# Writing 1/Q and its product with Q into the PSUM bank of h, in an attention, rational-MLP and expert kernel

## The chip, the cores and the metric

One core of one Trainium2 chip runs the whole program. The metric is device time in microseconds (us). The kernel before took 926.52 us, the median of 3 runs (925.81 to 928.81).

## The reference, cut to what matters

Three layers follow each other: causal attention with a window of 128 and a linear bias (4 batches, 8 heads, 576 tokens, 64 per head), a dense layer whose activation is a quotient of polynomials, and a top-1 mixture of 8 experts with ReLU. All is fp32. The change touches the quotient alone:

```python
h = x @ w_in                                  # 2304 tokens, 512 -> 2048
P = a[0] + a[1]*h + a[2]*h2 + a[3]*h3
Q = 1.0 + abs(b[0])*abs(h) + abs(b[1])*h2
g = P / (Q + 1e-06)
x = g @ w_out                                 # 2048 -> 512
```

## The kernel before

The 2304 tokens go in nine chunks of 256. For a chunk, `chunk_a` (L811) walks the 2048 columns of h in eight slots of 256 columns. This text counts these slots through the program, from 0 to 71; slots 0 to 7 are chunk 0. In a slot TensorE (PE) makes h with `up` (L478): two weight tiles with 12 matmuls each, three products (L482, L483, L484) for each quarter of the 512 inputs, because a value is carried as a rounded high part and the rest. They fill one tile `h_ps` of 128x512 fp32, a whole PSUM bank; its pool `ps_h` has two buffers, and all eight banks of PSUM are given out. So slot j+2 writes the bank that slot j wrote.

`rational` (L496) makes g of a slot on three other engines. ScalarE (ACT) takes ah = |h| (L503), u = c3 h + c2 (L504) and qq = b2 ah + b1 (L505); GpSimd (POOL) multiplies qq by ah (L508); ACT makes r0 = 1/Q as exp(-ln(qq + 1)) (L509, L510). VectorE (DVE) multiplies u by h (L511), adds c1 and multiplies by h (L512), adds c0 and multiplies by r0 (L515), makes (qq + 1) r0 (L518), and takes one Newton step (L521). ACT rounds the result to gh (L524) and POOL makes the rest gl (L525). u, qq and r0 have two buffers each, in SBUF. L503, L504, L511 and L512 are the only instructions that read the bank of h.

`down` (L486) multiplies gh and gl by the second half of the weights: 12 matmuls (L491, L492, L493) that add into two PSUM banks over a chunk. It runs two slots late (`LAG = 2`), so that PE's order is up(j+2), an attention piece, down(j), another attention piece, up(j+3):

```python
            run_slot(h)
            h_ps = ps_h.tile([P, 2, T], F32, name="h_ps")
            for i in range(2):
                up(w_res[2 * j + i], *xs[c], h_ps[:, i, :])
            run_slot(h + 1)
            if len(pend) >= LAG:
                flush()
            g = rational(h_ps)
```

`run_slot` issues pieces of the attention of a later chunk and of the routing of an earlier one, by a table that `plan_attention` and `routed` fill: scores (L340), transposes of the probabilities (L373), their product with v (L392), and on ACT and DVE the softmax, the rounding and splitting of q, k and x (L310 to L315, L399, L400), and copies out of PSUM (L378).

The order on each engine is a scheduler's, which follows a model of the time. From chunk 1 to chunk 8 PE is excepted (`tc.manual_schedule(engines={mybir.EngineType.PE})`): there it runs in the order in which the code is written. In chunk 0, whose slots also convert the weights, and in the expert stage the scheduler orders PE too. The tag `r0` of the pool `ep` also serves two setup tiles and a part of the expert weights in `load_split`.

Of the kernel before, what the change touches and what calls it, by code (L numbers as in the profile page):

```python
# [11 lines left out]
F32 = mybir.dt.float32  # L12
# [5 lines left out]
AF = mybir.ActivationFunctionType  # L18
ALU = mybir.AluOpType
# [4 lines left out]
P = 128  # L24
T = 256
# [18 lines left out]
def attention_rational_moe_kernel(  # L44
# [11 lines left out]
    nc = tc.nc  # L56
# [18 lines left out]
    ep = ctx.enter_context(tc.tile_pool(name="ep", bufs=2))  # L75
# [15 lines left out]
    co = const.tile([P, 6], F32, name="co")  # L91
# [3 lines left out]
    qc = const.tile([P, 1], F32, name="qc")  # L95
# [15 lines left out]
        out=upper, in_=ones, pattern=[[1, P]], compare_op=ALU.is_gt, fill=0.0,  # L111
# [11 lines left out]
    for h in range(H):  # L123
        sl = 2.0 ** (-8.0 * (h + 1) / H)
        nc.vector.tensor_scalar(
            out=bm[:, h, :], in0=rel, scalar1=-sl * D ** 0.5, scalar2=None, op0=ALU.mult
        )
        nc.gpsimd.affine_select(
            out=bm[:, h, :], in_=bm[:, h, :], pattern=[[-1, 2 * W]], compare_op=ALU.is_ge,
# [3 lines left out]
            out=bm[:, h, :], in_=bm[:, h, :], pattern=[[1, 2 * W]], compare_op=ALU.is_gt,  # L133
# [12 lines left out]
    def small_ps(i, n):  # L146
# [8 lines left out]
        out=tab.rearrange("(p r) c -> p (r c)", p=P), in_=fill.rearrange("p r c -> p (r c)")  # L155
# [340 lines left out]
    def rational(h_ps):  # L496
        u = ep.tile([P, 2, T], F32, name="u")
        ah = ahp.tile([P, 2, T], F32, name="ah")
        qq = ep.tile([P, 2, T], F32, name="qq")
        r0 = ep.tile([P, 2, T], F32, name="r0")  # L500
        gh = ep.tile([P, 2, T], F32R, name="gh", bufs=3)
        gl = ep.tile([P, 2, T], F32R, name="gl", bufs=3)
        nc.scalar.activation(out=ah, in_=h_ps, func=AF.Abs)  # L503
        nc.scalar.activation(out=u, in_=h_ps, func=AF.Identity, scale=co[:, 3:4], bias=co[:, 2:3])  # L504
        nc.scalar.activation(  # L505
            out=qq, in_=ah, func=AF.Identity, scale=babs[:, 1:2], bias=babs[:, 0:1]
        )
        nc.gpsimd.tensor_tensor(out=qq, in0=qq, in1=ah, op=ALU.mult)  # L508
        nc.scalar.activation(out=r0, in_=qq, func=AF.Ln, bias=qc)  # L509
        nc.scalar.activation(out=r0, in_=r0, func=AF.Exp, scale=-1.0)  # L510
        nc.vector.tensor_tensor(out=u, in0=u, in1=h_ps, op=ALU.mult)  # L511
        nc.vector.scalar_tensor_tensor(  # L512
            out=u, in0=u, scalar=co[:, 1:2], in1=h_ps, op0=ALU.add, op1=ALU.mult
        )
        nc.vector.scalar_tensor_tensor(  # L515
            out=u, in0=u, scalar=co[:, 0:1], in1=r0, op0=ALU.add, op1=ALU.mult
        )
        nc.vector.scalar_tensor_tensor(  # L518
            out=qq, in0=qq, scalar=qc, in1=r0, op0=ALU.add, op1=ALU.mult
        )  # L520
        nc.vector.scalar_tensor_tensor(  # L521
            out=u, in0=qq, scalar=2.0, in1=u, op0=ALU.subtract, op1=ALU.mult, reverse0=True
        )
        nc.scalar.copy(gh, u)  # L524
        nc.gpsimd.tensor_tensor(out=gl, in0=u, in1=gh.bitcast(F32), op=ALU.subtract)  # L525
        return gh, gl
# [277 lines left out]
    def chunk_a(c, att):  # L804
        for j in range(NF1 // 2):
            h = 16 * c + 2 * j
            if c == 0:
                convert(2 * j + 2 + LEAD)
# [8 lines that stand above are left out]
            then = 16 * (c + 1) + 5 if c + 1 < NCH else None  # L817
            pend.append((j, NF1 // 2, partial(routed, c, then), w_res[2 * j:2 * j + 2], *g))
            if j % 2 == 0:
                next(att, None)  # L820
            if c == NCH - 1 and j == JE:
                pick_early()
                early.append(prep(None))
            if c == NCH - 1 and j == JE + 2:
                early.append(turn(early.pop()))
# [63 lines left out]
```

## Time and profile before

| | before |
|---|---|
| median of 3 runs | 926.52 us |
| the profiled execution | 929.39 us |
| its span | 927.7 us |
| mean granted clock of TensorE | 0.967 |
| PE matmul, busy | 843.2 us (91%) |
| DVE, busy | 697.0 us (75%) |
| ACT, busy | 623.3 us (67%) |
| POOL, busy | 438.7 us (47%) |

Busy time is the time in which an engine executes; matmuls are pipelined, so that one of 128x256 shows some 290 ns while the next begins 120 ns after it. Idle time counts only on the engine that sets the end. The program has four stretches: the start with the attention of chunk 0 (to 69 us), slots 0 to 7 (69 to 123 us), slots 8 to 71 (123 to 656 us), and the experts, where PE is busy throughout (700 to 900 us).

### The profile page before, as it was taken

Reading aid. Unit: us, or ns where it says so; the run is one execution under the profiler, and the core shown is the slowest. Engines: PE = TensorE matmul, PEld = TensorE weight load, DVE = VectorE, ACT = ScalarE, POOL = GpSimd, SP = SyncE. Lnnn points to the kernel's source line nnn. Section 1 sums busy time; section 2 is a strip of 40 time slices with the busy share of each in tenths; the row PEclk is TensorE's granted clock in tenths of the full one; section 3 lists DMA queues with packets and bytes.
Section 4 is the critical chain, followed back from the end, with each engine's and each line's share of the span. In section 5 each row is a group of like instructions: output and inputs, shape, how many; then the busy total and the mean of one; then the engine's idle time right before and its main releaser. Section 6 shows DMA issues by size and latency. Waiting matters only on the chain. (4 is left out here: it accounts for less than half of the span.)

```text
span 927.7 us, 16232 instructions
## 1 busy us (share of the span) xinstructions
PE 843.2 (91%) x5550; PEld 727.5 (78%) x5550; DVE 697.0 (75%) x1415; ACT 623.3 (67%) x1300; POOL 438.7 (47%) x385
## 2 busy tenths in 40 slices
PE   4669998899899899989999999998969999999994
PEld 2348787778778788878788888887759999999993
DVE  7899997768998888987998988757646875555510
ACT  7999777667678678678778787764627755555510
POOL 3004354355455455454555464535547865555500
PEclk9999999889999999999999999998979999999998
DMA  8851213122122122212113121001448976668300
GB/s 320 288 196 46 82 42 86 44 47 81 43 54 86 37 66 69 61 44 69 49 45 92 38 68 39 1 23 47 115 143 306 316 245 228 227 227 273 125 6 20
DMA packets 69959, 101.88 MB, mean 110 GB/s; under 512 B 14705, under 2 KB 47345, under 8 KB 68082
## 3 DMA queue, kind: packets, MB, share of 16 engines
q1 hardware_dynamic: 64658, 86.11, 29.4%
q0 software_dynamic: 5216, 14.70, 4.5%
q8 instruction: 45, 0.74, 0.3%
q14 instruction: 40, 0.33, 0.1%
HBM read 91.13 MB, written 10.17 MB: 109 GB/s over the span
## 5 line engine op out<-in xcount | busy, mean ns | idle before, releaser
L482 PE MATMUL h_ps<-x,w 128*128 128x256 f32 x896 | 259.6, 291 | 7.9 <-ACT w L219 4.4
L483 PE MATMUL h_ps<-x,w 128*128 128x256 f32 x896 | 258.3, 288 | 0.5 <-DVE x L400 0.5
L484 PE MATMUL h_ps<-x,w 128*128 128x256 f32 x896 | 258.1, 288 | 0.1
L493 PE MATMUL y_ps<-w,gl 128*128 128x512 f32 x448 | 181.7, 409 | 13.3 <-POOL gl L525 13.1
L491 PE MATMUL y_ps<-w,gh 128*128 128x512 f32 x448 | 187.0, 417 | 3.3 <-ACT gh L524 3.2
L508 POOL TENSOR_TENSOR qq<-qq,ah 128x512 f32<-128x512 f32 x72 | 102.8, 1428 | 176.6 <-ACT qq L505 172.4
L482 PEld LDWEIGHTS h_ps<-x,w 128*128 128x128 f32 x896 | 175.1, 196 | 13.4 <-ACT w L219 4.7
L492 PE MATMUL y_ps<-w,gh 128*128 128x512 f32 x448 | 180.9, 404 | 0.0
L483 PEld LDWEIGHTS h_ps<-x,w 128*128 128x128 f32 x896 | 175.3, 196 | 4.1 <-DVE x L400 1.5
L484 PEld LDWEIGHTS h_ps<-x,w 128*128 128x128 f32 x896 | 175.7, 196 | 0.9 <-DVE w L240 0.4
L525 POOL TENSOR_TENSOR gl<-u,gh 128x512 fp32r<-128x512 f32 x72 | 99.0, 1376 | 117.6 <-ACT gh L524 85.5
L493 PEld LDWEIGHTS y_ps<-w,gl 128*128 128x128 f32 x448 | 87.6, 196 | 40.8 <-POOL gl L525 21.6
L240 POOL TENSOR_TENSOR w<-rawh,w 128x512 fp32r<-128x512 f32 x60 | 87.1, 1473 | 47.5 <-ACT w L239 47.3
L491 PEld LDWEIGHTS y_ps<-w,gh 128*128 128x128 f32 x448 | 88.1, 197 | 20.3 <-ACT gh L524 4.9
L492 PEld LDWEIGHTS y_ps<-w,gh 128*128 128x128 f32 x448 | 88.0, 197 | 15.2
L350 ACT ACTIVATE p_sb<-p_sb,nm 128x256 f32<-128x256 f32 (+4 forms) x160 | 74.9, 471 | 29.2 <-DVE nm L345 28.8
L315 POOL TENSOR_TENSOR qk<-k_sb,qk 128x384 fp32r<-128x384 f32 (+1 forms) x56 | 63.2, 1144 | 42.2 <-ACT qk L311 38.8
L524 ACT CAST gh<-u 128x512 fp32r<-128x512 f32 x72 | 44.4, 617 | 51.5 <-DVE u L521 50.7
L511 DVE TENSOR_TENSOR u<-u,h_ps 128x512 f32<-128x512 f32 x72 | 49.0, 681 | 30.6 <-ACT u L504 30.4
L518 DVE SCALAR_TENSOR_TENSOR qq<-qq,qc,r 128x512 f32<-128x512 f32 x72 | 71.4, 992 | 0.0
L515 DVE SCALAR_TENSOR_TENSOR u<-u,co,r 128x512 f32<-128x512 f32 x72 | 62.6, 869 | 11.4 <-ACT r L510 11.0
L345 DVE CUSTOM_DVE_ANT_0 p_sb<-s_ps,bm 128x256 f32<-128x256 f32 (+4 forms) x160 | 56.2, 372 | 18.3 <-PE s_ps L340 15.2
(141 smaller groups left out, 1567.4 us busy)
## 6 DMA issues: line engine op xcount, KB each, us to landing
rawh<-epack SPq DMA_DIRECT2D x100, 256.0 KB, 5.4
raw<-epack SPq DMA_DIRECT2D x30, 512.0 KB, 5.7
raw<-wpack SPq DMA_DIRECT2D x14, 1024.0 KB, 7.2
v_sb<-vv SPq DMA_DIRECT2D x92, 64.0 KB, 2.0
k_sb<-kT SPq DMA_DIRECT2D x28, 192.0 KB, 3.3
q_sb<-qT SPq DMA_DIRECT2D x40, 128.0 KB, 2.9
yd<-y_sb POOLq DMA_DIRECT2D x18, 256.0 KB, 2.9
k_sb<-kT SPq DMA_DIRECT2D x16, 160.0 KB, 3.1
```

Of the source, the lines that this page charges most:

```text
L240: (nc.gpsimd if i in POOLLO else nc.vector).tensor_tensor(out=w[:, 1, cs], in0=raw, in1=w[:, 0, cs].bitcast(F32), op=ALU.subtract)
L315: nc.gpsimd.tensor_tensor(out=kl, in0=k_sb[:, r, 0:kc], in1=kh.bitcast(F32), op=ALU.subtract)
L350: nc.scalar.activation(out=p_sb[0:L, r, 0:wn], in_=p_sb[0:L, r, 0:wn], func=AF.Exp, scale=-1.0, bias=nm[0:L, r:r + 1], accum_out=su[0:L, r ...
L482: nc.tensor.matmul(out_ps, w[:, 0, ws], xh[:, k, :], start=(k == 0), stop=False)
L483: nc.tensor.matmul(out_ps, w[:, 0, ws], xl[:, k, :], start=False, stop=False)
L484: nc.tensor.matmul(out_ps, w[:, 1, ws], xh[:, k, :], start=False, stop=(k == KD - 1))
L491: nc.tensor.matmul(y_ps[t], gh[:, i, ts], w[:, 0, DM:], start=a, stop=False)
L492: nc.tensor.matmul(y_ps[t], gh[:, i, ts], w[:, 1, DM:], start=False, stop=False)
L493: nc.tensor.matmul(y_ps[t], gl[:, i, ts], w[:, 0, DM:], start=False, stop=z)
L508: nc.gpsimd.tensor_tensor(out=qq, in0=qq, in1=ah, op=ALU.mult)
L518: nc.vector.scalar_tensor_tensor(out=qq, in0=qq, scalar=qc, in1=r0, op0=ALU.add, op1=ALU.mult)
L525: nc.gpsimd.tensor_tensor(out=gl, in0=u, in1=gh.bitcast(F32), op=ALU.subtract)
```

## The change

In `rational`, r0 is no longer a tile of its own: it is the bank of h. ln(Q) and 1/Q are written over h, once L511 and L512 (now L510 and L511) have read it, and (qq + 1) r0 is written there as well instead of over qq. The last three DVE instructions (now L516, L519, L522) then have one operand in SBUF and one in PSUM, where they had two in SBUF. The bank of h is read until L522. And qq is written ahead of u in the code, and L510 and L511 ahead of the logarithm (now L514).

```diff
-        r0 = ep.tile([P, 2, T], F32, name="r0")
+
+        r0 = h_ps
...
         nc.scalar.activation(out=ah, in_=h_ps, func=AF.Abs)
-        nc.scalar.activation(out=u, in_=h_ps, func=AF.Identity, scale=co[:, 3:4], bias=co[:, 2:3])
         nc.scalar.activation(
             out=qq, in_=ah, func=AF.Identity, scale=babs[:, 1:2], bias=babs[:, 0:1]
         )
+        nc.scalar.activation(out=u, in_=h_ps, func=AF.Identity, scale=co[:, 3:4], bias=co[:, 2:3])
         nc.gpsimd.tensor_tensor(out=qq, in0=qq, in1=ah, op=ALU.mult)
-        nc.scalar.activation(out=r0, in_=qq, func=AF.Ln, bias=qc)
-        nc.scalar.activation(out=r0, in_=r0, func=AF.Exp, scale=-1.0)
         nc.vector.tensor_tensor(out=u, in0=u, in1=h_ps, op=ALU.mult)
         nc.vector.scalar_tensor_tensor(
             out=u, in0=u, scalar=co[:, 1:2], in1=h_ps, op0=ALU.add, op1=ALU.mult
         )
+        nc.scalar.activation(out=r0, in_=qq, func=AF.Ln, bias=qc)
+        nc.scalar.activation(out=r0, in_=r0, func=AF.Exp, scale=-1.0)
         nc.vector.scalar_tensor_tensor(
             out=u, in0=u, scalar=co[:, 0:1], in1=r0, op0=ALU.add, op1=ALU.mult
         )
         nc.vector.scalar_tensor_tensor(
-            out=qq, in0=qq, scalar=qc, in1=r0, op0=ALU.add, op1=ALU.mult
+            out=r0, in0=qq, scalar=qc, in1=r0, op0=ALU.add, op1=ALU.mult
         )
         nc.vector.scalar_tensor_tensor(
-            out=u, in0=qq, scalar=2.0, in1=u, op0=ALU.subtract, op1=ALU.mult, reverse0=True
+            out=u, in0=r0, scalar=2.0, in1=u, op0=ALU.subtract, op1=ALU.mult, reverse0=True
         )
```

How the order moves is shown at three places. On ACT, slot 36, before (`h_ps_4387` is the bank of h of that slot, and `gh_4356` belongs to slot 35):

```order
L503 ACTIVATE ah_4432<-h_ps_4387 128x512
L524 CAST gh_4356<-u_4352 128x512
L504 ACTIVATE u_4431<-h_ps_4387,co_102 128x512
L378 COPY pt_sb_4413<-pt_ps_4412 128x512
L505 ACTIVATE qq_4433<-ah_4432,babs_104 128x512
L399 CAST x_4029<-x_ps_196 128x256
L509 ACTIVATE r0_4434<-qq_4433,qc_106 128x512
L310 CAST qk_4530<-q_sb_4326 128x256
```

And the same place of the change, where `h_ps_4351` is the bank and `gh_4320` belongs to slot 35:

```order
L525 CAST gh_4320<-u_4317 128x512
L504 ACTIVATE ah_4396<-h_ps_4351 128x512
L508 ACTIVATE u_4395<-h_ps_4351,co_102 128x512
L378 COPY pt_sb_4377<-pt_ps_4376 128x512
L505 ACTIVATE qq_4397<-ah_4396,babs_104 128x512
L399 CAST x_3996<-x_ps_196 128x256
L514 ACTIVATE h_ps_4351<-qq_4397,qc_106 128x512
L310 CAST qk_4493<-q_sb_4291 128x256
```

The rounding of the slot before moved ahead by one place. u (L504, now L508) stands ahead of qq in both, although the code now writes it behind: the scheduler puts u first in 56 of the 72 slots before, and in 70 of the 72 with the change. The logarithm now writes the bank and keeps its place.

On DVE, the last three instructions of slot 36, before:

```order
L604 TENSOR_TENSOR pick_4299<-x_ps_196,oh_4301 128x16
L605 TENSOR_REDUCE rk_4515<-pick_4299 128x2
L515 SCALAR_TENSOR_TENSOR u_4431<-u_4431,co_102,r0_4434 128x512
L518 SCALAR_TENSOR_TENSOR qq_4433<-qq_4433,qc_106,r0_4434 128x512
L609 TENSOR_TENSOR slot_4516<-rk_4515,pm_4300 128x2
L354 TENSOR_REDUCE ri_4464<-sum0_190 128x2
L521 SCALAR_TENSOR_TENSOR u_4431<-qq_4433,u_4431 128x512
```

With the change:

```order
L605 TENSOR_TENSOR pick_4264<-x_ps_196,oh_4266 128x16
L516 SCALAR_TENSOR_TENSOR u_4395<-u_4395,co_102,h_ps_4351 128x512
L519 SCALAR_TENSOR_TENSOR h_ps_4351<-qq_4397,qc_106,h_ps_4351 128x512
L606 TENSOR_REDUCE rk_4478<-pick_4264 128x2
L354 TENSOR_REDUCE ri_4427<-sum0_190 128x2
L522 SCALAR_TENSOR_TENSOR u_4395<-h_ps_4351,u_4395 128x512
```

They stand where they stood, and take their second operand from the bank.

On PE, chunk 0, the end of up of slot 2 and what follows, before (`h_ps_717` is slot 2, `h_ps_853` slot 3):

```order
L484 MATMUL h_ps_717<-x_236,w_524 128x256
L331 MATMUL s_ps_1023<-k_sb_991,q_sb_990 128x256
L331 MATMUL s_ps_1024<-k_sb_991,q_sb_990 128x256
L392 MATMUL x_ps_196<-pt_sb_796,v_sb_777 64x128 x4
L482 MATMUL h_ps_853<-x_236,w_638 128x256
```

With the change, where `h_ps_715` is slot 2 and `gh_557` slot 0:

```order
L484 MATMUL h_ps_715<-x_236,w_524 128x256
L491 MATMUL y_ps_740<-w_306,gh_557 128x512
L492 MATMUL y_ps_740<-w_306,gh_557 128x512
L493 MATMUL y_ps_740<-w_306,gl_558 128x512
```

The scheduler had run up of slot 3 ahead of down of slot 0; now down of slot 0 comes first, and so it goes on through chunk 0. From slot 9 to slot 71 PE's order is the same in both, row for row; it differs again only where the first expert chunk begins.

## Rows read from the trace of the kernel before

**Rows 1.** Stretches: start:end in us, then busy us (x instructions) by engine, clock, DMA.

```profile
core 0: us, PE busy (x) PEld busy (x) DVE busy (x) ACT busy (x) POOL busy (x), PEclk, DMA share, GB/s
69.00:123.00 54.00, 51.65 (x347) 42.40 (x347) 53.07 (x99) 45.80 (x93) 22.69 (x15) 1.00 0.23 66
123.00:656.00 533.00, 500.78 (x3481) 436.51 (x3480) 442.54 (x1003) 385.83 (x887) 263.92 (x215) 0.96 0.19 53
...
700.00:900.00 200.00, 200.00 (x1310) 182.90 (x1309) 115.91 (x123) 108.78 (x175) 119.80 (x88) 1.00 0.64 218
```

**Rows 2.** PE's waits, 123 to 656 us: who waited for whom, us, times, longest.

```profile
PE y_ps L493 <- POOL gl L525: 11.5, 13, 1.9
PE s_ps L340 <- DVE qk L312: 4.3, 4, 1.8
PE x_ps L560 <- DVE x L400: 3.2, 2, 1.6
PE pt_ps L729 <- DVE x L731: 2.9, 1, 2.9
...
PE y_ps L491 <- ACT gh L524: 1.4, 1, 1.4
```

**Rows 3.** Groups by line, whole program: busy us, mean ns, then idle before and releaser.

```profile
L508 POOL TENSOR_TENSOR qq<-qq,ah 128x512 f32<-128x512 f32 x72 | 102.8, 1428 | 176.6 <-ACT qq L505 172.4 <-PE y_ps L493 3.2 <-PE s_ps L340 0.7
L518 DVE SCALAR_TENSOR_TENSOR qq<-qq,qc,r 128x512 f32<-128x512 f32 x72 | 71.4, 992 | 0.0
L515 DVE SCALAR_TENSOR_TENSOR u<-u,co,r 128x512 f32<-128x512 f32 x72 | 62.6, 869 | 11.4 <-ACT r L510 11.0
L521 DVE SCALAR_TENSOR_TENSOR u<-qq,u 128x512 f32<-128x512 f32 x72 | 59.3, 823 | 0.7
L505 ACT ACTIVATE qq<-ah,babs 128x512 f32<-128x512 f32 x72 | 58.9, 819 | 0.1
L504 ACT ACTIVATE u<-h_ps,co 128x512 f32<-128x512 f32 x72 | 55.7, 774 | 3.2 <-POOL gl L525 3.0
L512 DVE SCALAR_TENSOR_TENSOR u<-u,co,h_ps 128x512 f32<-128x512 f32 x72 | 53.3, 741 | 1.1
```

**Rows 4.** Timeline, slot 36: start us, length us, engine, line; last matmul of its up.

```profile
381.23 0.28 PE L484 MATMUL h_ps<-x,w 128*128 128x256 f32 x1
...
385.24 0.75 DVE L512 SCALAR_TENSOR_TENSOR u<-u,co,h_ps 128x512 f32<-128x512 f32 x1
...
385.75 1.30 POOL L508 TENSOR_TENSOR qq<-qq,ah 128x512 f32<-128x512 f32 x1 [0.50 <-ACT qq L505]
...
387.08 0.72 ACT L509 ACTIVATE r<-qq,qc 128x512 f32<-128x512 f32 x1 [0.93 <-POOL qq L508]
...
389.64 0.62 ACT L510 ACTIVATE r<-r 128x512 f32<-128x512 f32 x1
...
392.50 0.68 DVE L521 SCALAR_TENSOR_TENSOR u<-qq,u 128x512 f32<-128x512 f32 x1
```

**Rows 5.** Timeline, PE: the first matmul of up of slot 38.

```profile
392.94 0.28 PE L482 MATMUL h_ps<-x,w 128*128 128x256 f32 x1
```

**Rows 6.** Timeline, slots 15 and 70: L521, and up two slots later.

```profile
217.16 0.69 DVE L521 SCALAR_TENSOR_TENSOR u<-qq,u 128x512 f32<-128x512 f32 x1
...
217.58 0.28 PE L482 MATMUL h_ps<-x,w 128*128 128x256 f32 x1
...
658.05 1.65 DVE L521 SCALAR_TENSOR_TENSOR u<-qq,u 128x512 f32<-128x512 f32 x1
...
656.24 0.36 PE L482 MATMUL h_ps<-x,w 128*128 128x256 f32 x1
```

**Rows 7.** Timeline, slots 18 and 71: L512 and the logarithm L509.

```profile
235.91 0.73 DVE L512 SCALAR_TENSOR_TENSOR u<-u,co,h_ps 128x512 f32<-128x512 f32 x1
...
235.65 0.72 ACT L509 ACTIVATE r<-qq,qc 128x512 f32<-128x512 f32 x1
...
660.73 0.75 DVE L512 SCALAR_TENSOR_TENSOR u<-u,co,h_ps 128x512 f32<-128x512 f32 x1
...
660.89 0.72 ACT L509 ACTIVATE r<-qq,qc 128x512 f32<-128x512 f32 x1 [0.42 <-POOL qq L508]
```

## The prediction

> **What bounds the kernel now.** I read the busy time by stretch first. From 700 to 900 us PE is busy without a gap [rows 1], so whatever delays the stretch before it delays the end. From 123 to 656 us, which is slots 8 to 71, PE is busy for 500.8 of 533 us and DVE for 442.5 (83%) [rows 1]. PE leads, but not by much: 533 us for 64 slots is 8.33 us a slot. The second view is PE's waits in that stretch: all its waits together are 31.7 us, and the largest is down's third matmul for gl, 11.5 us; with 1.4 us for gh that is 12.9 us [rows 2]. So PE sets the pace, and what holds it up most often is the end of the rational chain. The third view is the chain itself in one slot, read along the timeline. In slot 36, up ends at 381.51 (381.23 and 0.28), L512 reads the bank of h last at 385.99, and L521 ends at 393.18 [rows 4]: 4.5 us and 11.7 us behind up. Lined up in the same way, the 64 slots have a mean of 12.8 us from the end of up to the end of L521. Up of slot 38, which takes the same bank, begins at 392.94 [rows 5], 7 us after L512 and 0.24 us before the end of L521. That is the point on which I decide: today the bank is free long before PE comes for it; with the change it is free about when PE comes.
>
> **The change part by part.**
>
> *Three DVE instructions lose their second SBUF operand.* L518 takes 992 ns on average, L515 869 and L521 823, while L512, which has the same shape with one operand in PSUM, takes 741 [rows 3]; an L521 with POOL idle takes 0.68 us [rows 4]. The excess is 0.25, 0.13 and 0.14 us, 0.52 us a slot, 37 us of DVE time over 72 slots. I give the change all of it (its other end is nothing). DVE is not the bound, so this counts as a shorter chain only.
>
> *POOL's product qq by ah* takes 1428 ns on average [rows 3] and 1.30 us where DVE leaves it alone [rows 4]: 0.13 us a slot off the chain (between nothing and that).
>
> *ACT and DVE writing to PSUM.* No row shows it. On the reading side, u from PSUM takes 774 ns and qq from SBUF 819 [rows 3], 45 ns apart; for writes I allow the same either way, at most 0.09 us a slot for two ACT writes, and take nothing. The DVE write is bounded by the same 0.05 us and taken at nothing.
>
> *qq ahead of u* would let POOL start 0.77 us sooner. It does not happen: in the scheduled order of ACT, u stands ahead of qq in 70 of 72 slots. Nothing.
>
> *The logarithm has to wait until L512 has read h.* In slot 36 it costs nothing: L512 ends at 385.99, and L509 begins at 387.08, released by POOL [rows 4]. In 23 of the 64 slots L509 began before L512 had ended, in slot 18 by 1.0 us (235.65 against 236.64), in slot 71 by 0.6 us [rows 7]; with 0.07 us from one engine to the next these are 25.6 us, 1.1 us each. There ACT stands still, and behind the logarithm in its queue are the roundings of q and k (L310, L311), on which POOL, DVE and later PE's scores wait. I count it as a longer chain in those slots.
>
> *The bank is held until L521 (now L522).* This is the largest term. In 26 of the 64 slots up of slot j+2 began before L521 of slot j had ended, from slot 15 by 0.26 us (217.58 against 217.84) to slot 70 by 3.47 us (656.24 against 659.70) [rows 6]; with 0.1 us for the hand-over, 54.8 us in all. PE runs in written order here, so up can't be passed: behind it stand an attention piece, down(j) and the next up, and ACT, DVE and POOL wait for these in turn. The sum overstates it: if up(j) was already late, its chain is late, and a slot between adds only what exceeds the delay already gathered. Taking for each up the larger of the delay of the up before it and of (delay of up(j) plus the lateness of slot j) gives 46.8 us. With each slot's own excess on the three DVE instructions taken off it is 32.2 us, and with the logarithm's wait added 34.2 us, in 27 late slots.
>
> *What that takes the place of.* Down(j) comes right behind up(j+2), so a PE that has waited for L522 waits less for gh and gl: minus 12.9 us [rows 2]. The 0.13 us of POOL in 27 late slots: minus 3.4 us. A DVE with less to do also shortens PE's waits for L312, L400 and L731, 10.4 us [rows 2]; I take a quarter, minus 2.6 us (from nothing to all).
>
> *Chunk 0.* There all eight ups begin before L521 of the slot two back has ended, and down(0) now stands ahead of up(3). But DVE is busy for 53.1 of 54 us [rows 1]: it is the bound, it has a little less to do, and a late up costs nothing as long as DVE has other work in its queue, which the conversion of the weights gives it. I take 0. Without that cover, the same running sum through the slots of chunk 0 adds 20 us.
>
> *The rest.* In the expert stage nothing of `rational` runs. The tag r0 now serves the expert weights without waiting for `rational`; PE is busy throughout there, so that hides it. The order of SP's transfers hardly changes, and POOL's scatters keep their places among its products.
>
> Sum: 34.2 - 12.9 - 3.4 - 2.6 + 0 = 15.3 us. On the profiled execution (929.4 us, of which the span is 927.7) that is 944.7; it was 2.9 us above the median of 926.5, so the forecast for the median is 941.8 us, slower by 1.7%.
>
> One rule would make another sum. The Trainium skill (Perfetto Trace Analysis, Identifying the Most-Contended Engine) says that PE's matmul busy time is no good measure, that its weight loads are to be taken instead, and that the engine with the highest occupancy is to be relieved first; the weight loads are busy for 436.5 us in slots 8 to 71 and DVE for 442.5, so by it DVE binds. By the same page's Optimization Strategy, a gap that repeats can mean too few PSUM buffers, which is the mechanism of my sum; no gap of that kind stands in this trace yet.
>
> **The rivals.**
>
> *The shorter chain outweighs the bank (faster).* Its place is down(j): gl comes sooner by the 0.65 us of DVE and POOL, and if queues empty as well, fewer ups are late. The same running sum with 1.5 us more off every slot leaves 15.7 of the 34.2 us, and with 2.5 us more 8.6. Against these go the 12.9 us for gh and gl and, with DVE freer, half of the 10.4 us: 8.6 - 12.9 - 5.2 = -9.5, about 917 us. It decides from some 1.5 us, a mean chain of about 11 us. For it: a PE that waits lets ACT and DVE catch up, and PE's waits feed on the same queues. Against it: the direct gain is 0.65 us, and the logarithm's wait takes 0.4 us of that back on average. Chance 0.20.
>
> *DVE is the bound.* In slots 8 to 71 the excess on its three instructions is 34.8 us; if DVE set the pace, all of that would go: 892 us. Against it, DVE is idle for 90 of the 533 us and PE's waits for DVE and POOL together are under 30 us. Chance 0.05.
>
> *Nothing changes.* The ups that come late are those behind which PE would have waited anyway, and the gains pay for the rest: 34.2 would have to fall to some 19 us. 926.5 us. Chance 0.12.
>
> *Chunk 0 is not covered, and the chain's relief brings nothing.* 20 us on top of the forecast: 962 us. Chance 0.05.
>
> **How the numbers follow.** The forecast, PE waiting at up, has 0.58. Of its own terms, the 34.2 us lie between 15.7 (a further 1.5 us off the chain) and 46.8 (no relief at all), so by itself, with the same 12.9 and 2.6 us against it, it reaches from some 927 to 954. The range of eight in ten has to take in the faster rival: 917 to 960. It leaves out the DVE bound (0.05), the uncovered chunk 0 (0.05) and a little at each end. What a measurement of this kernel can tell from no change is about 0.3%, 2.8 us. Faster: 0.20 and 0.05, 0.25. Same: 0.12. Slower: 0.58 and 0.05, 0.63.
>
> **What would show it.** In the changed profile L516, L519 and L522 should all last 0.68 to 0.76 us with no long ones, and DVE's busy time should fall by about 37 us. L514 should be released by DVE (L511) in about a third of the slots. The first matmul of up (L482) should show waits for DVE's L522, some 25 to 35 us in all, and the waits for gl and gh should nearly vanish. If L522 hardly appears among PE's waits, the chain became shorter than I think and the faster rival holds; if it appears but the time doesn't move, those waits only changed their name. If slots 0 to 7 last over 5 us longer, my cover by DVE in chunk 0 was wrong.

## The result, and the profile after

The change is slower: 941.38 us, the median of 4 runs (936.83 to 942.64), against 927.33 us before (4 runs, 925.81 to 928.81). The ratio is 1.0143, with a 95% interval of 1.0104 to 1.0181. The profiled execution took 941.67 us, its span 939.9 us, with a mean granted clock of 0.959 (0.967 before).

The stretches of the changed kernel that answer to [rows 1]; slots 0 to 7 now end at 130.4 us and slots 8 to 71 at 667.1 us:

```profile
69.00:130.40 61.40, 54.05 (x354) 45.05 (x354) 56.41 (x109) 47.58 (x97) 21.01 (x16) 0.94 0.22 62
130.40:667.10 536.70, 498.82 (x3486) 441.81 (x3485) 399.45 (x999) 387.16 (x888) 253.78 (x217) 0.96 0.19 52
712.00:912.00 200.00, 200.00 (x1310) 182.85 (x1309) 117.70 (x123) 108.86 (x175) 117.79 (x86) 1.00 0.64 218
```

DVE fell from 442.5 to 399.5 us in slots 8 to 71, and the stretch still became longer, by some 3.4 us (533.3 to 536.7 from the first matmul of slot 8 to that of the experts). In front of it, the slots of chunk 0 begin at 18.8 us in both, and slot 8 begins 7.5 us later. The 3.4 us are what is left of gains and losses: by the table of chunks under e7, chunk 1 became 9.4 us shorter, chunks 2 to 5 together 0.9 us shorter, and chunks 6 to 8 together 13.8 us longer.

PE's waits from 130.4 to 667.1 us, which answer to [rows 2]:

```profile
PE h_ps L482 <- DVE u L522: 26.1, 11, 4.4
PE h_ps L482 <- DVE cnt L640: 3.0, 1, 3.0
PE x_ps L583 <- DVE x L400: 1.9, 1, 1.9
PE s_ps L340 <- DVE qk L312: 1.5, 1, 1.5
PE y_ps L493 <- POOL gl L526: 1.4, 3, 0.7
...
PE s_ps L340 <- POOL qk L315: 1.1, 3, 0.5
PE h_ps L482 <- DVE ri L354: 0.5, 1, 0.5
```

A wait that did not exist before, of up for L522, is now the largest by far. The two other waits of up, put down to cnt (L640) and ri (L354), end within 0.15 us behind the L522 that frees the bank, so they are probably the same wait: 29.6 us with them. The waits for gl fell from 11.5 to 1.4 us, and that for gh is gone.

The same view by chunks shows where the new wait costs time. PE's largest waits in chunks 2 to 5, two rows of before (209.82 to 478.32 us), then two of the change (207.87 to 475.43 us):

```profile
PE y_ps L493 <- POOL gl L525: 8.1, 7, 1.9
PE x_ps L560 <- DVE x L400: 3.2, 2, 1.6
...
PE h_ps L482 <- DVE u L522: 13.2, 5, 4.4
PE y_ps L493 <- POOL gl L526: 1.0, 2, 0.7
```

And all of them in chunks 6 to 8, three rows of before (478.32 to 656.24 us), then four of the change (475.43 to 667.10 us):

```profile
PE y_ps L493 <- POOL gl L525: 3.4, 6, 0.9
PE pt_ps L729 <- DVE x L731: 2.9, 1, 2.9
PE y_ps L491 <- ACT gh L524: 1.4, 1, 1.4
...
PE h_ps L482 <- DVE u L522: 12.9, 6, 3.8
PE h_ps L482 <- DVE cnt L640: 3.0, 1, 3.0
PE pt_ps L730 <- DVE x L732: 1.4, 1, 1.4
PE y_ps L493 <- POOL gl L526: 0.4, 1, 0.4
```

In chunks 2 to 5 the wait for the bank took the place of waits that were there before, and the length hardly changed. In chunks 6 to 8 there was little to take the place of: the waits rose from 7.7 to 17.7 us.

The groups of the changed kernel that answer to [rows 3]:

```profile
L482 PE MATMUL h_ps<-x,w 128*128 128x256 f32 x896 | 266.5, 298 | 45.3 <-DVE u L522 32.5 <-ACT w L219 4.4 <-ACT w L239 3.3
...
L509 POOL TENSOR_TENSOR qq<-qq,ah 128x512 f32<-128x512 f32 x72 | 96.4, 1339 | 214.4 <-ACT qq L505 214.2
...
L519 DVE SCALAR_TENSOR_TENSOR h_ps<-qq,qc,h_ps 128x512 f32<-128x512 f32 x72 | 53.8, 747 | 0.0
...
L516 DVE SCALAR_TENSOR_TENSOR u<-u,co,h_ps 128x512 f32<-128x512 f32 x72 | 53.4, 741 | 20.6 <-ACT h_ps L515 20.1
L514 ACT ACTIVATE h_ps<-qq,qc 128x512 f32<-128x512 f32 x72 | 49.7, 690 | 33.1 <-POOL qq L509 22.6 <-DVE u L511 5.3 <-DVE pick L574 2.0
L522 DVE SCALAR_TENSOR_TENSOR u<-h_ps,u 128x512 f32<-128x512 f32 x72 | 49.3, 685 | 0.7
```

The three DVE instructions take 741, 747 and 685 ns instead of 869, 992 and 823, and the longest of them lasts 752 ns, where it was 2268 ns before. The Trainium skill (SBUF — State Buffer, Who interferes with whom) says that a DVE instruction with two SBUF inputs contends with a GpSimd instruction that reads SBUF, and that one with at most one, outside the modes that use two ports, does not contend with GpSimd; these rows agree. The logarithm waits for L511 for 5.3 us in all, in 5 places; two more of its waits, of 1.5 and 1.8 us and put down to other DVE instructions, end the same 0.1 us behind L511, so that it may be 8.6 us in 7.

Where up waits longest is shown by the timeline of DVE in the changed kernel. L519 at 230.56 and L522 at 234.05 belong to slot 17:

```profile
230.56 0.75 DVE L519 SCALAR_TENSOR_TENSOR h_ps<-qq,qc,h_ps 128x512 f32<-128x512 f32 x1
231.22 0.74 DVE L511 SCALAR_TENSOR_TENSOR u<-u,co,h_ps 128x512 f32<-128x512 f32 x1
231.88 0.41 DVE L345 CUSTOM_DVE_ANT_0 p_sb<-s_ps,bm 128x256 f32<-128x256 f32 x1
232.22 0.08 DVE L345 DVE_READ_ACCUMULATOR2_ANT nm<- 128x1 f32 x1
232.22 0.42 DVE L400 TENSOR_TENSOR x<-x_ps,x 128x256 fp32r<-128x256 f32 x1
232.56 0.41 DVE L345 CUSTOM_DVE_ANT_0 p_sb<-s_ps,bm 128x256 f32<-128x256 f32 x1
232.90 0.08 DVE L345 DVE_READ_ACCUMULATOR2_ANT nm<- 128x1 f32 x1
233.01 1.01 DVE L312 TENSOR_TENSOR qk<-q_sb,qk 64x256 fp32r<-64x256 f32 x1
234.05 0.69 DVE L522 SCALAR_TENSOR_TENSOR u<-h_ps,u 128x512 f32<-128x512 f32 x1
```

On PE at that time:

```profile
234.79 0.58 PE L482 MATMUL h_ps<-x,w 128*128 128x256 f32 x1 [3.84 <-DVE u L522]
```

L519 ends at 231.31, and the scheduler put seven instructions of other work between it and L522. The bank stays taken until 234.74, and up of slot 19 waits 3.84 us. The same happens to up of slots 27, 35, 51 and 59, two slots behind 25, 33, 49 and 57, where seven, seven, five and seven instructions stand there: 4.37, 3.84, 1.91 and 3.84 us. These five are 17.8 of the 26.1 us.

The matmuls behind a wait of that length are slow. The stretches of the changed kernel from 231 to 245 us:

```profile
231.00:234.00 3.00, 0.00 (x0) 0.00 (x0) 2.97 (x8) 3.00 (x9) 2.74 (x3) 0.99 0.22 66
234.00:241.00 7.00, 6.21 (x30) 6.21 (x31) 4.04 (x9) 2.34 (x6) 2.56 (x2) 0.51 0.37 95
241.00:245.00 4.00, 4.00 (x27) 3.57 (x27) 3.20 (x13) 3.12 (x6) 1.30 (x1) 1.00 0.01 1
```

PE stood still from 231.0 to 234.8. From 234 to 241 us the granted clock is 0.51, the lower of its two levels, 1.2 GHz, and 30 matmuls take 6.21 us of busy time; from 241 us, back at 2.4 GHz, 27 take 4.00. Behind each of the other four waits there is such a stretch too, of 3.4 to 6.8 us at 0.50 or 0.51 (from 302.2, 367.1, 503.6 and 568.5 us). The kernel before has them as well, behind shorter waits: 0.51 from 305.8 to 309 us, 2 us after a wait of 1.6 us. Over slots 8 to 71 the clock is 0.96 in both.

### The profile page after: what moved, and what is told of

It is laid out like the page before. It is cut to its first block, busy times and chain, and to the rows that moved or that the text cites. A ratio compares the mean times of both kernels' runs of the same rounds, so it can differ in the third digit from the quotient of the medians.

```text
span 939.9 us, 16343 instructions
## 1 busy us (share of the span) xinstructions
PE 842.1 (90%) x5550; PEld 735.7 (78%) x5550; DVE 652.4 (69%) x1415; ACT 622.8 (66%) x1300; POOL 423.5 (45%) x385
## 3 DMA queue, kind: packets, MB, share of 16 engines
q1 hardware_dynamic: 64658, 86.11, 28.9%
## 5 line engine op out<-in xcount | busy, mean ns | idle before, releaser
L482 PE MATMUL h_ps<-x,w 128*128 128x256 f32 x896 | 266.5, 298 | 45.3 <-DVE u L522 32.5
L483 PE MATMUL h_ps<-x,w 128*128 128x256 f32 x896 | 263.7, 294 | 0.5 <-DVE x L400 0.5
L484 PE MATMUL h_ps<-x,w 128*128 128x256 f32 x896 | 263.5, 294 | 0.0
L482 PEld LDWEIGHTS h_ps<-x,w 128*128 128x128 f32 x896 | 180.3, 202 | 54.3 <-DVE u L522 29.3
L509 POOL TENSOR_TENSOR qq<-qq,ah 128x512 f32<-128x512 f32 x72 | 96.4, 1339 | 214.4 <-ACT qq L505 214.2
L483 PEld LDWEIGHTS h_ps<-x,w 128*128 128x128 f32 x896 | 181.1, 202 | 4.0 <-DVE x L400 1.5
L491 PE MATMUL y_ps<-w,gh 128*128 128x512 f32 x448 | 182.7, 408 | 0.0
L484 PEld LDWEIGHTS h_ps<-x,w 128*128 128x128 f32 x896 | 181.5, 203 | 0.4
L493 PE MATMUL y_ps<-w,gl 128*128 128x512 f32 x448 | 176.1, 396 | 1.4 <-POOL gl L526 1.4
L492 PE MATMUL y_ps<-w,gh 128*128 128x512 f32 x448 | 177.2, 396 | 0.0
L491 PEld LDWEIGHTS y_ps<-w,gh 128*128 128x128 f32 x448 | 85.9, 192 | 15.2 <-issue 0.2
L492 PEld LDWEIGHTS y_ps<-w,gh 128*128 128x128 f32 x448 | 86.0, 192 | 14.3
L510 DVE TENSOR_TENSOR u<-u,h_ps 128x512 f32<-128x512 f32 x72 | 49.0, 681 | 62.1 <-ACT u L508 61.9
L315 POOL TENSOR_TENSOR qk<-k_sb,qk 128x384 fp32r<-128x384 f32 (+1 forms) x56 | 59.0, 1071 | 33.2 <-ACT qk L311 21.6
L514 ACT ACTIVATE h_ps<-qq,qc 128x512 f32<-128x512 f32 x72 | 49.7, 690 | 33.1 <-POOL qq L509 22.6
L516 DVE SCALAR_TENSOR_TENSOR u<-u,co,h_ps 128x512 f32<-128x512 f32 x72 | 53.4, 741 | 20.6 <-ACT h_ps L515 20.1
L240 DVE TENSOR_TENSOR w<-raw,w 128x1024 fp32r<-128x1024 f32 x30 | 47.3, 1578 | 26.7 <-ACT w L239 26.7
```

The costliest lines, as they stand in the source:

```text
L240: (nc.gpsimd if i in POOLLO else nc.vector).tensor_tensor(out=w[:, 1, cs], in0=raw, in1=w[:, 0, cs].bitcast(F32), op=ALU.subtract)
L315: nc.gpsimd.tensor_tensor(out=kl, in0=k_sb[:, r, 0:kc], in1=kh.bitcast(F32), op=ALU.subtract)
L482: nc.tensor.matmul(out_ps, w[:, 0, ws], xh[:, k, :], start=(k == 0), stop=False)
L483: nc.tensor.matmul(out_ps, w[:, 0, ws], xl[:, k, :], start=False, stop=False)
L484: nc.tensor.matmul(out_ps, w[:, 1, ws], xh[:, k, :], start=False, stop=(k == KD - 1))
L491: nc.tensor.matmul(y_ps[t], gh[:, i, ts], w[:, 0, DM:], start=a, stop=False)
```

## The experiments

My theory was that of the forecast: the held bank makes the loss, and the relief of DVE pays back a part. The rivals were that the scheduler's new order makes it, that the logarithm's new wait makes it, and that relief is worth nothing. All ratios are to the kernel before on the same chip. The experiments ran on three chips (e1 to e4, e5 to e8, e9 to e11), so where kernels of different groups, or one of them and the change, are compared, the ratios count.

**e1, the order of the code alone.**

```diff
-        r0 = h_ps
+        r0 = ep.tile([P, 2, T], F32, name="r0")
...
-            out=r0, in0=qq, scalar=qc, in1=r0, op0=ALU.add, op1=ALU.mult
+            out=qq, in0=qq, scalar=qc, in1=r0, op0=ALU.add, op1=ALU.mult
...
-            out=u, in0=r0, scalar=2.0, in1=u, op0=ALU.subtract, op1=ALU.mult, reverse0=True
+            out=u, in0=qq, scalar=2.0, in1=u, op0=ALU.subtract, op1=ALU.mult, reverse0=True
```

> The change's order of the code alone: r0 back in its SBUF tile, (qq+1) r0 back in qq, so that the bank of h is free after L511 as before and the last three DVE instructions have two SBUF operands. Theory (the held bank makes the loss): no wait of up for L522 at all, long DVE instructions (up to 1.8 us) as before, 924 to 931 us. Rival (the new order that the scheduler makes is what costs): 935 to 942 us.

928.18 us, ratio 1.0009 (0.9982 to 1.0036). Writing qq ahead of u, and L510 and L511 ahead of the logarithm, does nothing by itself.

**e2, an attempt to hold the bank alone** (the kernel before, with two lines more).

```diff
+        held = sm.tile([P, 1], F32, name="held")
+        nc.vector.tensor_copy(held, h_ps[:, 0, 0:1])
         nc.scalar.copy(gh, u)
```

> The kernel before, and behind the Newton step a DVE copy of one column out of the bank of h, which does nothing but keep the bank until then; r0 stays in SBUF, nothing is relieved. The copies themselves are 72 of under 0.1 us on DVE. Theory (holding costs, relief gives some of it back): slower than the change, 948 to 970 us, waits of up for DVE over 40 us in all. Rival (order): 926 to 933 us. A second rival (the held bank costs only what the waits for gl cost before): 930 to 940 us.

921.07 us, ratio 0.9934 (0.991 to 0.9957), below all three ranges, and no wait of up for the copy. The experiment failed: the copy depends on h alone, and the scheduler put it right behind L512, so nothing was held. It measures something else: 72 tiny instructions, which relieve nothing and with which the scheduler orders the work anew, move the time by 0.7%. A difference of that size between two of these kernels says little about the cause that it was made for.

**e5, the bank really held.**

```diff
+        held = sm.tile([P, 1], F32, name="held")
+        nc.vector.tensor_tensor(out=held, in0=u[:, 0, 0:1], in1=h_ps[:, 0, 0:1], op=ALU.mult)
         nc.scalar.copy(gh, u)
```

> As e2, but the small DVE instruction behind the Newton step multiplies one column of u by one column of the bank of h, so that the scheduler can't put it ahead of L521 as it did with the copy of e2: the bank is really held, r0 stays in SBUF, nothing is relieved. Theory (holding the bank makes the loss, and the relief pays for a part of it): 945 to 968 us, up waits for this instruction for over 40 us in all. Rival (the bank's waits only take the place of other waits, and the loss comes from something else in the change): 920 to 936 us.

970.8 us, ratio 1.0485 (1.0435 to 1.0536), a little above the range. PE's waits, the first row, and slots 8 to 71 of this kernel:

```profile
PE h_ps L482 <- DVE held L525: 42.2, 15, 5.4
```

```profile
133.03:696.74 563.71, 508.12 (x3486) 449.57 (x3486) 440.50 (x1062) 391.61 (x888) 261.67 (x218) 0.94 0.18 50
```

Holding the bank costs some 46 us when nothing pays for it, net of the waits that it takes the place of, and give or take the 0.7% of e2. The mean granted clock of this kernel is 0.942.

**e4 and e3, relief without holding.** Both put the scores of a pair's two heads into one PSUM bank; e4 keeps r0 in SBUF, e3 gives r0 the bank that became free, from chunk 1 on.

```diff
-    ps_s = ctx.enter_context(tc.tile_pool(name="ps_s", bufs=2, space=PSUM))
+    ps_s = ctx.enter_context(tc.tile_pool(name="ps_s", bufs=1, space=PSUM))
+    ps_r = ctx.enter_context(tc.tile_pool(name="ps_r", bufs=1, space=PSUM))
...
-        s_ps = [ps_s.tile([P, 2 * W], F32, name="s_ps") for _ in range(2)]
+        both = ps_s.tile([P, 2, 2 * W], F32, name="s_ps")
+        s_ps = [both[:, 0], both[:, 1]]
+        if c < PACK:
+            s_ps[1] = ps_r.tile([P, 2, T], F32, name="r_ps")[:, 0]
```

and in e3 alone:

```diff
-        r0 = h_ps
+        r0 = ps_r.tile([P, 2, T], F32, name="r_ps") if bank else ep.tile([P, 2, T], F32, name="r0")
+        q1 = r0 if bank else qq
```

where `bank` is `c >= 1`, and q1 takes the place of r0 as the output of L519 and the first input of L522. e3 is made from the change and e4 from the kernel before, so that e3 also has the change's order of the code, which by e1 does nothing.

> The kernel before with the scores of both heads in one PSUM bank and the other bank left to the second head of the first two chunks alone: the control of e3, r0 in SBUF. Both theories: 926 to 940 us, the cost of one bank less for the scores, as waits of the scores (L340) for DVE's softmax (L345).

> r0 and (qq+1) r0 in a PSUM bank of their own from chunk 1 on (chunk 0 keeps the SBUF tile): relief without holding the bank of h. The bank is won by putting the scores of both heads of a pair into one bank instead of two; the two heads' first chunks still use two. Against e4, which has the same scores and r0 in SBUF. Theory: DVE's three instructions at 0.68 to 0.76 us, no waits of up for DVE, faster than e4 by 6 to 15 us; if the shared score bank costs little, 912 to 922 us. Rival (the relief is worth nothing, PE is the bound): equal to e4 within 3 us.

e4: 920.73 us, ratio 0.9928 (0.9896 to 0.9959), faster where I had expected a cost; by e2 that is within what a new order does. e3: **898.66 us, ratio 0.9688 (0.9653 to 0.9723)**, 22 us below e4, where I had expected 6 to 15, and below the range of 912 to 922 too. Slots 8 to 71 of e4, then of e3:

```profile
122.80:649.70 526.90, 494.64 (x3482) 433.68 (x3480) 435.45 (x1006) 386.62 (x890) 266.13 (x215) 0.97 0.20 54
```

```profile
122.10:621.90 499.80, 484.55 (x3482) 427.29 (x3481) 401.16 (x1006) 383.56 (x888) 249.35 (x215) 0.99 0.21 56
```

DVE has 34 us less to do, and the stretch is 27 us shorter. Of these, 17 us are idle time of PE (32.3 to 15.3 us) and 10 us its busy time, at a clock of 0.99 in place of 0.97. So relief is worth something although PE leads, three times what a new order did in e2; in the change the held bank ate it.

**e6, the bank free after L519.**

```diff
-            out=r0, in0=qq, scalar=qc, in1=r0, op0=ALU.add, op1=ALU.mult
+            out=qq, in0=qq, scalar=qc, in1=r0, op0=ALU.add, op1=ALU.mult
...
-            out=u, in0=r0, scalar=2.0, in1=u, op0=ALU.subtract, op1=ALU.mult, reverse0=True
+            out=u, in0=qq, scalar=2.0, in1=u, op0=ALU.subtract, op1=ALU.mult, reverse0=True
```

> The change, but (qq+1) r0 goes back to qq in SBUF, so that the bank of h is free after L519 and not after L522, some 1.2 us earlier; L522 has two SBUF operands again (0.14 us longer on average). Theory (the length of the hold counts): waits of up for DVE fall from 32 to 12 to 20 us, 926 to 937 us. Rival (the logarithm's wait or the order makes the loss): 938 to 945 us.

905.27 us, ratio 0.9778 (0.973 to 0.9827): 36 us less than the change, or 34 by the ratios, where I had expected 4 to 15. Slot 17 of this kernel, on DVE and on PE:

```profile
226.55 0.74 DVE L519 SCALAR_TENSOR_TENSOR qq<-qq,qc,h_ps 128x512 f32<-128x512 f32 x1
...
229.64 1.39 DVE L522 SCALAR_TENSOR_TENSOR u<-qq,u 128x512 f32<-128x512 f32 x1
```

```profile
227.39 0.34 PE L482 MATMUL h_ps<-x,w 128*128 128x256 f32 x1
```

L522 stands nearly as far behind L519 as in the change (2.35 us against 2.74), with the same seven instructions between, but up of slot 19 begins 0.1 us after L519. My 1.2 us, an average, hid that in four of the five slots above L522 ends 3.4 us behind L519. PE's waits for L519 are now small, and the granted clock in slots 8 to 71 rises to 0.99:

```profile
PE y_ps L493 <- POOL gl L526: 6.8, 9, 2.3
PE h_ps L482 <- DVE qq L519: 4.3, 4, 1.7
```

```profile
128.29:636.12 507.83, 486.45 (x3494) 427.98 (x3493) 415.51 (x1001) 388.12 (x892) 260.49 (x217) 0.99 0.20 55
```

**e7, e9 and e10, the bank in some chunks only.** `rational` takes a flag and uses the SBUF tile where it is false.

```diff
-            g = rational(h_ps)
+            g = rational(h_ps, c >= 1)
```

e9 has `1 <= c <= 5` there; e10 is e6 with `c >= 1`.

> The change from chunk 1 on; chunk 0 keeps r0 in SBUF and its bank free after L511. Theory (chunk 0 costs 7.5 us by itself): slots 0 to 7 take 104 us again instead of 112, and the whole 931 to 937 us. Rival (chunk 1 gives back what chunk 0 loses, it was 9.4 us shorter in the change): 938 to 944 us, with chunk 1 at 84 to 87 us again.

> The change in chunks 1 to 5 alone; chunks 0 and 6 to 8 keep r0 in SBUF. In the change chunks 1 to 5 were 10.4 us shorter than before, chunks 0 and 6 to 8 21.3 us longer. Theory (these are places where the held bank binds or doesn't: late in the attention a slot is shorter, and the chain no longer fits into two of them): 914 to 924 us. Rival (the order that the scheduler makes as a whole decides, and a part of it can't be taken alone): 926 to 940 us.

> The kernel of e6 (bank free after L519) from chunk 1 on, chunk 0 with r0 in SBUF. Theory (chunk 0's loss is apart from the rest, as e7 showed): 5 us less than e6, 897 to 903 us. Rival (chunk 1 takes it back): 903 to 908 us.

The length of a chunk, from the first matmul of up in its first slot to that of the next chunk, in the profiled executions (us; the weights of chunk 0 begin to be used at 18.8 us in all):

| chunk | before | change | e7 | e9 | e6 | e10 |
|---|---|---|---|---|---|---|
| 0 | 104.1 | 111.7 | 103.7 | 103.7 | 109.5 | 103.6 |
| 1 | 86.9 | 77.4 | 81.0 | 82.8 | 76.2 | 80.6 |
| 2 to 5 | 268.5 | 267.6 | 269.4 | 268.8 | 254.1 | 254.1 |
| 6 to 8 | 177.9 | 191.7 | 190.9 | 177.8 | 177.6 | 179.5 |

e7: 936.03 us, ratio 1.0107 (1.0057 to 1.0158), inside the range. Chunk 0 took 8.0 us less than in the change, and chunk 1 took 3.6 us of that back; by the ratios the whole is 3.3 us faster than the change, and the two intervals overlap. e9: 924.72 us, ratio 0.9971 (0.9949 to 0.9993), 0.7 us above the range: chunks 6 to 8 are back at 177.8 us, but chunk 1 lost 5.4 us against the change and chunks 2 to 5 gained nothing. From e7 to e9 the bank goes out of chunks 6 to 8 as well; they become 13.1 us shorter and the whole 12.6 us faster by the ratios. So the change's net loss over the kernel before lies mostly there. e10: 905.12 us, ratio 0.9779 (0.9744 to 0.9814), the same as e6 within the interval: here chunk 1 took 4.4 of 5.9 us back, and the rival of that experiment held. So chunk 0's loss is real, but a good part of it is work that chunk 1 would have to do.

**e8, the logarithm's wait alone**, on the code of e1.

```diff
+        qd = sm.tile([P, 1], F32, name="qd")
+        nc.vector.tensor_scalar(out=qd, in0=u[:, 0, 0:1], scalar1=0.0, scalar2=1.0 + 1e-6, op0=ALU.mult, op1=ALU.add)
-        nc.scalar.activation(out=r0, in_=qq, func=AF.Ln, bias=qc)
+        nc.scalar.activation(out=r0, in_=qq, func=AF.Ln, bias=qd)
```

> The kernel of e1, with the logarithm's bias computed from one column of u behind L511 by a DVE instruction of one column: the logarithm waits for L511 as in the change, and for a small instruction more; the bank is not held, nothing is relieved. Theory: a few us, 927 to 934 us. Rival (this wait makes the loss of the change): 938 to 950 us, with ACT waiting for DVE at the logarithm for over 25 us.

948.71 us, ratio 1.0241 (1.0192 to 1.029): the rival's range, but not its sign. ACT stood idle for the small instruction for 3.8 us only, in 7 places, where the rival had over 25. Two of PE's waits in it:

```profile
PE y_ps L493 <- POOL gl L528: 14.8, 23, 1.1
PE y_ps L491 <- ACT gh L527: 13.3, 11, 2.4
```

This kernel is some 20 us above e1. On average the small instruction begins 1.0 us behind L511, and the logarithm 8.1 us behind up in place of 6.8 in e1; how much of the 20 us is this and how much the new order is not shown. In the change itself the logarithm waited for L511 for 5.3 to 8.6 us, and e6, which has this wait too, is 2.2% faster than before; so it isn't what makes the change slow.

**e11, the own bank, freed early**: e3 with `q1 = qq`.

> The kernel of e3 (r0 in a bank of its own) with (qq+1) r0 back in SBUF, so that this single bank comes free for the next logarithm after L519 instead of L522, and L522 has two SBUF operands. Theory (the own bank is not waited for, so that only the contention of L522 comes back): 898 to 906 us, no better than e3. Rival (the logarithm waits for the bank in e3): 888 to 896 us.

910.2 us, ratio 0.9824 (0.9786 to 0.9862), 12 us worse than e3 and above both ranges. L522 with two SBUF operands again takes 806 ns on average in place of 685. That the logarithm waits for the single bank in e3 is not borne out; why some 9 us more of DVE time (654.1 to 662.9 us) cost 12 us here stays open; a new order may be part of it.

## Why the prediction came out as it did

**The sum was right, its split was not.** I had 15.3 us in slots 8 to 71 and nothing elsewhere. The trace of the change has 3.4 us in slots 8 to 71, 7.5 us in chunk 0 and the remaining 1.3 us at the change-over to the experts, where the bank of slot 71 makes an up wait for 2.5 us. Steps that were off cancelled: that the median came out within 0.4 us of 941.8 is luck. The direction, and the wait of up for L522 as its cause, are not.

**Chunk 0, "I take 0": wrong.** DVE was to cover a late up there with other work. e7 shows that it does not: without the bank in chunk 0 it is 8.0 us shorter. Chunk 1 covers a good part afterwards: the whole is 3.3 us faster by the ratios in e7, and no faster in e10 than in e6. The uncovered end of 20 us was too high.

**The held bank, 34.2 us: right in kind, near in size.** Up waited for L522 for 26.1 us in slots 8 to 71 (29.6 with the two waits that are probably the same) and for 32.5 us in all. The slots that were late before [rows 6] are not all the same ones that wait now. e5 shows the hold without relief, 46 us; the forecast's own terms for that, 46.8 less 12.9, make 33.9. But I read it as a matter of the chain's length, with a point of decision at a mean of about 11 us. The mean from the end of up to the end of the Newton step did fall to 10.8 us, and the faster rival still failed: the waits sit in 11 of 64 ups, above all where L522 stands behind five or seven other instructions. What decides is how long the longest chains are, and that is an order, which I had in front of me and did not read for this. And I set the new waits against the old ones over the whole stretch, where they meet chunk by chunk: they pay for each other in chunks 2 to 5 and do not in chunks 6 to 8, where e9 shows the loss. Why the gain of chunk 1 does not stay without the bank in chunk 0 is open.

**The relief, 0.65 us a slot: too small.** The instructions became as short as I said (DVE 697.0 to 652.4 us), POOL gave less (1428 to 1339 ns), but the chain became 2.0 us shorter. Of these, 1.75 us lie ahead of the end of L511, behind which the three instructions of the slot stand: its mean distance from the end of up fell from 6.1 to 4.4 us. In e5, where nothing is relieved and PE waits, it is 4.7 us, and in e6, where PE hardly waits at up, 5.3. So a PE that waits, as the faster rival said, and the relief each bring it about; their shares in the change were not separated. e3 against e4 gives 22 us for relief alone.

**The waits for gl and gh, minus 12.9 us: right,** 12.9 to 1.4 us. **PE's other waits, minus 2.6 us: too small.** All but those two and the waits for L522 went from 18.8 to 10.2 us, and to 6.7 without the two that are probably for L522.

**The logarithm: too large.** 25.6 us of ACT's time in 23 slots became 5.3 us in 5, or 8.6 in 7, in the whole program; L511 came 1.75 us sooner behind up. **u ahead of qq: right,** as e1 shows.

**A term that I left out: the clock.** Lost clock, the span times one minus the mean, is 927.7 x 0.033 = 30.6 us before, 939.9 x 0.041 = 38.5 in the change, 968.5 x 0.058 = 56.2 in e5, 902.2 x 0.021 = 18.9 in e6. Some of it falls where PE is idle or waits anyway, so these are upper bounds, but they move with the time: up to 8 us of the 12.2 us between before and the change, and up to 20 of the 37.7 us between the change and e6. In slots 8 to 71 the clock is 0.96 before and in the change, so little of the 8 us arises there; from the change to e6 it rises to 0.99, and 536.7 x 0.04 = 21.5 against 507.8 x 0.01 = 5.1 is up to 16 of the 28.9 us by which that stretch is shorter. No experiment separated the clock from the waits.

**The rivals.** That DVE is the bound fails for the change; but with the bank not held, e3 comes to 898.7 us where that rival had 892. It gets there another way: DVE is idle for 98.6 of the 499.8 us in slots 8 to 71 of e3, and 17 of the 27 us gained on e4 are idle time of PE. The rule that stood beside it (the Trainium skill, Perfetto Trace Analysis, Identifying the Most-Contended Engine) pointed at the engine whose relief did pay.

**Slips of the working.** The own range of the forecast's terms, with 12.9 and 2.6 us against 46.8, ends at 958 and not at 954, which has the 3.4 us for POOL in it too. Of the 26 late slots two are late only by the 0.1 us for the hand-over. In [rows 4] POOL begins a scatter at 392.80 us, inside the L521 that was read as one with POOL idle. None of these moves the sum.

## What to carry to other kernels

Before an operand moves into a buffer that another engine waits for, line up the last read of every slot with the next write, and look at the longest cases and at what the scheduler put between the last two reads, not at the mean. A buffer should be let go by the instruction that is first able to: here one operand put back into SBUF (e6) turned 1.4% slower into 2.2% faster, and a bank of its own (e3) into 3.1%, of which the shared score bank (e4) is 0.7%. A new wait is free only where it stands in for an old one, and that differs from stretch to stretch. When a scheduler makes the order, a control without the effect has to be run too: e2 moved the time by 0.7% with nothing in it.

## What I had not expected of the hardware

A long wait of PE was followed by matmuls at the lower clock in all five cases above. After PE had stood idle for 3.8 us the granted clock was 0.51 from 234 to 241 us, as shown above; in the whole of e5 it was 0.942, in e6 0.979. The net cost is smaller than one such wait suggests, since the shorter waits of the kernel before left slots 8 to 71 at the same 0.96.

ACT writes to PSUM a little faster than to SBUF: the logarithm took 690 ns in place of 721, and the exponential, which now also reads there, 583 in place of 625. I had allowed for either sign and taken nothing. DVE showed no such difference: L519 took 747 ns into PSUM and 740 ns into SBUF in e6.
